# Blocks of 512 queries, a slot softmax behind the loop, and a list scheduler, in attention followed by a soft mixture of experts

## The chip, the cores and the metric

The kernel runs on one core of a Trainium2 chip. PE is TensorE (matrix products), DVE is VectorE, ACT is ScalarE, POOL is GpSimd, and SP issues DMA transfers. Each engine works through its own list of instructions in order and waits on semaphores for the others. The metric is the device time of one execution in microseconds (us), as the median of three runs.

## The reference

q has 4 batches of 12288 queries with 128 channels. Keys and values are the same 768 vectors per batch: kv pooled 4 by 4, times w_sr. Attention is followed by a soft mixture of experts with 32 slots (8 experts of 4):

```python
kv_flat = kv_pool.reshape(B, -1, C) @ w_sr      # k = v, 768 x 128 per batch
s = scale * (q @ k.transpose(0, 2, 1))
a = np.exp(s - s.max(-1, keepdims=True)); a /= a.sum(-1, keepdims=True) + 1e-09
x = (a @ v).reshape(B * N, C)                   # 49152 x 128
logits = x @ phi                                # 49152 x 32
d = softmax of logits over all rows             # dispatch
slot_out = experts(d.T @ x)                     # relu(. @ w1) @ w2
c = softmax of logits over the 32 slots         # combine
out = c @ slot_out
```

## The kernel before, in words

**Blocks and steps.** The queries go through in 192 blocks of 256. Of each block the scores are made transposed, 768 keys in six tiles of 128 on the partitions, queries along the free axis (`qk`, L289 to L291: three products per tile, since keys and queries are split into a high and a low part). The score tiles s lie in three PSUM tiles of one bank each, each with two buffers: six of the eight banks. The remaining two hold everything else (`pm`, tag m).

The row maximum crosses partitions. DVE takes a maximum of every 32 by 32 square while it transposes it (`rowmax1`, L301, result r), reduces over tiles (L309), multiplies by a pattern (L314, result rq), PE spreads this over the partitions (`rowmax_pe`, L322, result pq), DVE reduces again (L327) and transposes it into mb (L332). It subtracts mb from the scores into t in SBUF (`sub_part`, L342). ACT takes the exponential twice (L352 into 16-bit phi, L353 into 32-bit t), POOL subtracts the two into plo (L362), and PE multiplies phi and plo with the values and with values times the router phi (`av`, L377, L378, L380, result px; 161 columns: a row sum, 128 channels, 32 logits). ACT copies px into xl (L393). Query splits: ACT copies q into qhi, POOL makes qlo (L272), 512 queries at a time.

**Groups.** Every 2048 queries form a group (steps `g0` to `g7`): logits L, their running maximum mrun (L489), the weights D (POOL, L495 and L514) and the dispatch sum pd (PE, L555), added to acc with rescaling. The combine softmax is made per group, too (steps `k3`, `k5`, `k6`, `k8`): maximum and sum over slots on DVE (L477, L524), subtraction and multiplication on POOL (L480, L536), four transposes on PE (L567), copied into cT. The last 2048 queries are two small groups whose steps run on DVE.

**Batches.** Keys and values of the next batch are summed by accumulating transfers on POOL's queue, the last halves by POOL itself (`kv_fold`). PE makes K (pk) and V (pv), DVE klo.

**Order.** The order is written out by hand: PROG lists the steps of a block with lags, and group and batch steps are hung in at fixed block numbers. PE, DVE, ACT and POOL keep the order in which the program records.

**Behind the loop** come the experts (ph, pso), the split of the slot outputs, and the output: 25 chunks, each with 12 products on PE (po, L799), four evacuations on DVE and ACT, a high/low split (chi, clo) on ACT and POOL, and its transfer.

## Time and profile before

| what | value |
|---|---|
| median of 3 runs | 1234.87 us (1234.6 to 1235.92) |
| profiled execution: its time, its span | 1237.04 us, 1235.3 us |
| PE, DVE, POOL, ACT busy | 1119.8, 1093.4, 913.2, 859.1 us |
| granted TensorE clock, mean over the span | 0.983 |
| first scores, first expert product, first output product | 21.05, 1144.30, 1158.83 us |

The span runs from the first to the last instruction of the profiled execution; its time has what lies around it as well. Busy times of one engine are a union of its instructions. Ends of PE instructions are modelled, so the distance between starts says more of PE than durations do.

### The profile page before, as it was taken

To read this page: it belongs to the slowest core of one execution; us is meant where nothing else is said; L and a number is where in the kernel's file an instruction comes from. 1 tells how busy PE (TensorE), PEld (TensorE's weight loads), DVE (VectorE), ACT (ScalarE), POOL (GpSimd) and SP (SyncE) were. 2 spreads that over 40 slices of the span, in tenths; PEclk is the share of its full clock that TensorE was granted. 3 is DMA by queue.
4 is the path that set the end of the run, shared out by engine and by line. 5 is a ranking of instruction groups with operands and counts; after the bars stand their busy time and mean duration, and the time that the engine had idled before them with its cause. 6 is when DMAs were issued, how large, how long until landed. Compare 5 with 4: busy or idle time off the path is not lost.

```text
span 1235.3 us, 29414 instructions
## 1 busy us (share of the span) xinstructions
PE 1119.8 (91%) x12120; PEld 1062.9 (86%) x12120; DVE 1093.4 (89%) x2369; ACT 859.1 (70%) x1042; POOL 913.2 (74%) x498
## 2 busy tenths in 40 slices
PE   3799999988999999998999999998999999996897
PEld 2699989988989989988989999987989999996586
DVE  6899999988999999989999999889999999998454
ACT  1577777766777777866777777776777877775364
POOL 0478888976788888976888879966888778775242
PEclk9799999999999999999999999999999999999899
DMA  9113230210133220210132310210110110013398
GB/s 353 60 34 92 58 77 2 86 36 1 36 73 66 59 63 2 87 35 2 35 87 53 83 39 2 86 36 1 36 35 2 36 35 2 35 36 104 106 370 341
DMA packets 19446, 85.92 MB, mean 70 GB/s; under 512 B 1648, under 2 KB 7024, under 8 KB 13424
## 3 DMA queue, kind: packets, MB, share of 16 engines
q1 hardware_dynamic: 12064, 56.37, 12.8%
q0 software_dynamic: 2448, 14.16, 6.1%
q10 hardware_dynamic: 4800, 13.52, 2.8%
q8 instruction: 96, 1.57, 0.5%
q14 instruction: 38, 0.31, 0.1%
HBM read 58.87 MB, written 25.17 MB: 68 GB/s over the span
## 4 chain that ended last, share of the span: by engine, by line
PE 50%; DVE 43%; ACT 3%; issue 2%; DMA 1%; DVEq 0%; SPq 0%
DVE r L301 14%; DVE t L342 11%; PE px L380 9%; PE px L377 8%; PE px L378 8%; PE po L799 5%; PE s L289 4%; PE s L291 4%; PE s L290 4%; PE pq L322 3%; DVE mrun L489 2%; DVE rq L314 2%; DVE cm L455 2%; DVE mb L332 2%; PE pd L555 2%
## 5 line engine op out<-in xcount | busy, mean ns | idle before, releaser
L362 POOL TENSOR_TENSOR plo<-t,phi 128x1536 f16<-128x1536 f32 x192 | 602.9, 3140 | 185.0 <-ACT t L353 71.9
L301 DVE TRANSPOSE_TENSOR_REDUCE r<-s 128x16 f32<-128x512 f32 x576 | 406.5, 706 | 12.5 <-PE s L291 9.7
L342 DVE TENSOR_TENSOR t<-s,mb 128x512 f32<-128x512 f32 x576 | 362.1, 684 | 16.9
L377 PE MATMUL px<-vhi,phi 128*128 128x161 f16 x2304 | 360.8, 235 | 0.3 <-DVE c L469 0.3
L378 PE MATMUL px<-vlo,phi 128*128 128x160 f16 x2304 | 360.7, 234 | 0.0
L289 PE MATMUL s<-qhi,khi 128*128 128x256 f32 x1152 | 344.0, 299 | 6.0 <-DVE t L342 5.5
L290 PE MATMUL s<-qlo,khi 128*128 128x256 f32 x1152 | 325.8, 283 | 0.0
L291 PE MATMUL s<-qhi,klo 128*128 128x256 f32 x1152 | 325.2, 282 | 0.4 <-DVE klo L183 0.4
L352 ACT ACTIVATE phi<-t,lnk 128x1536 f16<-128x1536 f32 (+1 forms) x193 | 301.4, 1562 | 22.0 <-DVE t L342 22.0
L353 ACT ACTIVATE t<-t,lnk 128x1536 f32<-128x1536 f32 (+1 forms) x193 | 302.9, 1569 | 6.3
L393 ACT ACTIVATE xl<-px 128x322 f32<-128x322 f32 x192 | 84.5, 440 | 259.3 <-PE px L380 203.6
L377 PEld LDWEIGHTS <-phi 128*128 128x128 f16 x2304 | 242.4, 105 | 0.0
L380 PE MATMUL px<-vhi,plo 128*128 128x161 f16 x2304 | 230.7, 235 | 0.0
L289 PEld LDWEIGHTS s<-qhi,khi 128*128 128x128 f32 x1152 | 219.7, 191 | 12.3 <-issue 7.0
L378 PEld LDWEIGHTS <-phi 128*128 128x128 f16 x2304 | 226.5, 98 | 0.3 <-issue 0.3
L290 PEld LDWEIGHTS s<-qlo,khi 128*128 128x128 f32 x1152 | 219.7, 191 | 0.9 <-issue 0.7
L291 PEld LDWEIGHTS s<-qhi,klo 128*128 128x128 f32 x1152 | 219.3, 190 | 0.7 <-DVE klo L183 0.7
L380 PEld LDWEIGHTS <-plo 128*128 128x128 f16 x2304 | 176.9, 99 | 0.2 <-DVE plo L362 0.2
L272 POOL TENSOR_TENSOR qlo<-q,qhi 128x512 fp32r<-128x512 f32 x96 | 126.7, 1321 | 56.6 <-ACT qhi L270 56.6
L322 PE MATMUL pq<-rq,sel 128*128 128x32 f32 x384 | 73.2, 273 | 71.7 <-DVE rq L314 71.2
L322 PEld LDWEIGHTS pq<-rq,sel 128*128 128x128 f32 x384 | 57.6, 189 | 92.1 <-issue 34.6
L332 DVE STREAM_TRANSPOSE mb<-m 128x256 f32<-128x256 f32 x192 | 77.2, 402 | 0.0
(134 smaller groups left out, 1084.7 us busy)
## 6 DMA issues: line engine op xcount, KB each, us to landing
q<-qT SPq DMA_DIRECT2D x23, 1024.0 KB, 4.9
...
```

What stands on the lines that cost most here:

```text
L289: nc.tensor.matmul(s[:, t, :], khi[:, ks], hi[:, sl], start=True, stop=False)
L290: nc.tensor.matmul(s[:, t, :], khi[:, ks], lo[:, sl], start=False, stop=False)
L291: nc.tensor.matmul(s[:, t, :], klo[:, ks], hi[:, sl], start=False, stop=True)
L301: nc.vector.tensor_reduce(out=MX[i][:, t0 : t0 + n, :], in_=S[i][h].rearrange("p t (b j) -> p t b j", j=Q32), axis=X, op=ALU.max, apply_tr ...
L322: nc.tensor.matmul(pqv, sel, MX[i].rearrange("p k b -> p (k b)"), start=True, stop=True)
L342: nc.vector.tensor_tensor(out=t[:, t0 : t0 + n, :], in0=S[i][k], in1=m.unsqueeze(1).broadcast_to([P, n, BQ]), op=ALU.subtract)
L352: nc.scalar.activation(hi[:, k : k + n, :], tk, AF.Exp, bias=lnk, scale=SCALE)
L353: nc.scalar.activation(tk, tk, AF.Exp, bias=lnk, scale=SCALE)
L362: (nc.vector if k else nc.gpsimd).tensor_tensor(out=lo[:, sl, :], in0=t[:, sl, :], in1=PP[i][:, sl, :], op=ALU.subtract)
L377: nc.tensor.matmul(px3[:, k, :], hi[:, t, ks], vhi[:, t, :], start=(t == 0), stop=False)
L378: nc.tensor.matmul(px3[:, k, 1:], hi[:, t, ks], vlo[:, t, :], start=False, stop=False)
L380: nc.tensor.matmul(px3[:, k, :], lo[:, t, ks], vhi[:, t, :], start=False, stop=(t == NT - 1))
```

## The change

**Blocks and tiles.** A block has 512 queries, so there are 96 of them. The three score tiles have two banks each and one buffer. One DVE instruction takes a maximum over two banks (1024 elements a partition), and subtractions are 1024, 512, 512 and 1024 wide, since t is now made of half blocks of three key tiles (three buffers). Exponentials and plo work on a half block: the same size as before (128 x 1536), and as many of them. The two remaining banks m0 and m1 are handed out by the planner; pq and its small result use the top columns of a bank beside px. Query splits are 512 wide as before, one for each block.

**Planner.** Each step is recorded with an engine, a cost, a due time, its dependencies and the buffers that it takes. `Plan.emit` then simulates the engines and writes out the steps: at each engine it takes, of what could start within 0.12 us, the step with the smallest due time; steps of the row maximum are marked hot and go first.

**Moved work.** The combine softmax keeps all logits in LL and runs group by group, but its steps depend on the last subtraction of the loop (end_) and have the last due times. The transposes read LL by chunk, in the output stage, and clo is made by DVE, straight from PSUM. `kv_fold` is two accumulating transfers instead of POOL's additions. The group maximum is taken with one transposing reduction, and gm stays in PSUM. The last group pair is 1536 and 512 queries. All output transfers go through SP. The first query load has 512 columns, as before, but this is now one block.

```diff
+AVD = 2.0
+HOLD = 0.7
+URGE = 60.0
...
+        def best(e):
+            found = []
+            for n in avail[e]:
+                t = acquire(n, free[e])
+                if t is not None:
+                    found.append((max(free[e], ready[n], t), ops[n][3], n))
+            if not found:
+                return None
+            t0 = min(found)[0] + 0.12
+            hot = [f for f in found if ops[f[2]][9]]
+            if hot:
+                h = min(hot)
+                if h[0] - t0 < HOLD:
+                    fits = [(p, t, n) for t, p, n in found if t <= t0 and t + ops[n][1] <= h[0] + 0.1]
+                    return min(fits) if fits else (h[1], h[0], h[2])
+            return min((p, t, n) for t, p, n in found if t <= t0)
...
-    BQ = 256
+    BQ = 512
...
+    NH = 2
+    TH = NT // NH
+    PB = 5
+    TBUF = 3
...
-    ps = es.enter_context(tc.tile_pool(name="ps", bufs=2, space=PSUM))
-    pm = es.enter_context(tc.tile_pool(name="pm", bufs=2, space=PSUM))
+    ps = es.enter_context(tc.tile_pool(name="ps", bufs=1, space=PSUM))
+    pm = es.enter_context(tc.tile_pool(name="pm", bufs=1, space=PSUM))
...
+    LL = cp.tile([P, NB * TB, NS], F32, tag="LL", name="LL")
+    RM = cp.tile([P, NB * TB], F32, tag="RM", name="RM")
...
+    banks = [pm.tile([P, 512], F32, tag=f"m{b}", name=f"m{b}") for b in range(2)]
+
+    def mt(shape, name):
+        return banks[plan.bank]
...
     def kv_fold(b, h):
-        yield POOL_
         t = kvs[b]
-        if h == 0:
-            nc.gpsimd.tensor_tensor(out=t[:, 0:2, :], in0=t[:, 0:2, :], in1=t[:, 2:4, :], op=ALU.add)
-        else:
-            pooled[b] = bp.tile([P, NK], F32, tag="pooled", name=f"pooled_{b}", bufs=1)
-            nc.gpsimd.tensor_tensor(out=pooled[b], in0=t[:, 0, :], in1=t[:, 1, :], op=ALU.add)
...
+        n = 2 - h
+        nc.gpsimd.dma_start(out=t[:, :n, :], in_=t[:, n : 2 * n, :], accum_op=ALU.add, max_dma_last_dim=4 * 2 * NK)
+        if h:
+            pooled[b] = t[:, 0, :]
...
+    def qk(i, t):
+        khi, klo = kT[i // BPB]
+        hi, lo = qsp[i]
+        if t % 2 == 0:
+            S[i, t // 2] = ps.tile([P, 2, BQ], F32, tag=f"s{t // 2}", name=f"s_{i}_{t // 2}")
+        s = S[i, t // 2][:, t % 2, :]
+        ks = slice(t * P, (t + 1) * P)
+        nc.tensor.matmul(s, khi[:, ks], hi, start=True, stop=False)
+        nc.tensor.matmul(s, khi[:, ks], lo, start=False, stop=False)
+        nc.tensor.matmul(s, klo[:, ks], hi, start=False, stop=True)
...
+    def rowmax1(i, u):
+        if u == 0:
             MX[i] = sp.tile([P, NT, NBK], F32, tag="r6", name=f"r6_{i}")
-        t0, n = SG[h]
         nc.vector.tensor_reduce(
-            out=MX[i][:, t0 : t0 + n, :], in_=S[i][h].rearrange("p t (b j) -> p t b j", j=Q32), axis=X,
+            out=MX[i][:, 2 * u : 2 * u + 2, :].rearrange("p t b -> p (t b)"),
+            in_=S[i, u].rearrange("p t (b j) -> p (t b) j", j=Q32), axis=X,
             op=ALU.max, apply_transpose=True,
         )
...
+        top = banks[plan.bank][:, 512 - (NQD + 1) * NBK :]
+        pq = PQ[i] = top[:, NBK:]
+        r1 = top[:, :NBK]
...
+    def sub(i, t, n):
+        h, o = divmod(t, TH)
+        if o == 0:
+            TT_[i, h] = sp.tile([P, TH, BQ], F32, tag="t", name=f"t_{i}_{h}", bufs=TBUF)
+        u = t % 2
         nc.vector.tensor_tensor(
-            out=t[:, t0 : t0 + n, :], in0=S[i][k], in1=m.unsqueeze(1).broadcast_to([P, n, BQ]), op=ALU.subtract
+            out=TT_[i, h][:, o : o + n, :], in0=S[i, t // 2][:, u : u + n, :],
+            in1=MX[i].unsqueeze(1).broadcast_to([P, n, BQ]), op=ALU.subtract,
         )
...
+        d["gm"] = d["pc"][:, NS : 2 * NS]
         nc.vector.transpose(out=d["gm"], in_=c1.broadcast_to([P, NS]))
...
+    def k_max(g):
+        o, n = GB[g][0] * TB, nt(g)
+        nc.vector.tensor_reduce(out=RM[:, o : o + n], in_=LL[:, o : o + n, :], axis=X, op=ALU.max)
...
+        o, n = GB[g][0] * TB, nt(g)
+        c = LL[:, o : o + n, :]
+        nc.gpsimd.tensor_tensor(out=c, in0=c, in1=bc(RM[:, o : o + n], NS), op=ALU.subtract)
...
+    def k_rec(g):
+        o, n = GB[g][0] * TB, nt(g)
+        r = RM[:, o : o + n]
+        nc.vector.tensor_scalar_add(r, r, EPS)
+        nc.vector.reciprocal(out=r, in_=r)
...
+        if n == 3:
+            ops["qr", 0] = op("SP", 0.5, 28.0, 0, [loaded[-1]], lambda: q_load(0, BQ, GQ))
...
+        pe = op("PE", 0.27, 0.3, T0 - 10, [r2], lambda i=i: rowmax_pe(i), use=[("m", ("pq", i)), ("rq", i)], hot=True)
...
+        for t, n in ((0, 2), (2, 1), (3, 1), (4, 2)):
...
+        a = op("DVE", dve(n), 0.08, p, [ops["L", g]] + end_, lambda g=g: k_max(g))
+        a = op("POOL", n / 512, 0.1, p, [a, ops["g4", g]], lambda g=g: k_sub(g))
+        a = op("ACT", act(n), 0.1, p, [a], lambda g=g: k_exp(g))
+        a = op("DVE", dve(n), 0.08, p, [a], lambda g=g: k_sum(g))
+        a = op("DVE", 0.3, 0.08, p, [a], lambda g=g: k_rec(g), raw=0.14)
+        ops["c", g] = op("POOL", n / 512, 0.1, p, [a], lambda g=g: k_mul(g))
...
+    def c_t(g):
+        o, n = chunks[g]
+        pt = U[g, "pt"] = mt([P, 512], f"pt_{g}")
+        for j in range(n):
+            k = (o + j) * TS
+            nc.tensor.transpose(out=pt[:, j * P : (j + 1) * P], in_=LL[:, k : k + TS, :], identity=ident)
...
+    def c_lo(g):
+        n = chunks[g][1] * P
+        nc.vector.tensor_tensor(out=U[g, "lo"], in0=U[g, "pt"][:, :n], in1=U[g, "hi"].bitcast(F32), op=ALU.subtract)
```

**PE around the row maximum** (m is one of the two shared banks, pq in it; phi, plo: the block two steps back). Before, the end of a block's scores:

```order
L290 MATMUL s_4_9418<-qlo_9097,khi_8141 128x256
L291 MATMUL s_4_9418<-qhi_9096,klo_8142 128x256
L322 MATMUL pq_9404<-rq_9406,sel 128x32 [waits DVE_49,PE_49]
L377 LDWEIGHTS phi_9198
L377 MATMUL px_9426<-vhi_8724,phi_9198 128x161 [waits Activation_49]
```

and after, in block 53, where 30 px matmuls stand between the scores and these rows:

```order
L528 LDWEIGHTS phi_1_7357
L528 MATMUL m_113<-vlo_6004,phi_1_7357 128x160
L479 MATMUL m_112<-rq_7560,sel 128x64 [waits DVE_49,Activation_49]
L535 LDWEIGHTS plo_0_7410
L535 MATMUL m_113<-vhi_6003,plo_0_7410 128x161
```

pq moved from the end of the scores (of the block before, by lag) to behind one and two thirds of the four px tiles of the same turn.

**POOL at the start.** Before:

```order
L272 TENSOR_TENSOR qlo_126<-q_111,qhi_125 128x512
L272 TENSOR_TENSOR qlo_208<-q_111,qhi_207 128x512
L272 TENSOR_TENSOR qlo_210<-q_111,qhi_209 128x512
L362 TENSOR_TENSOR plo_295<-t_258,phi_269 128x1536
L272 TENSOR_TENSOR qlo_311<-q_111,qhi_310 128x512
```

and after:

```order
L442 TENSOR_TENSOR qlo_133<-q_117,qhi_132 128x512
L512 TENSOR_TENSOR plo_0_248<-t_0_234,phi_0_242 128x1536
L512 TENSOR_TENSOR plo_1_251<-t_1_240,phi_1_246 128x1536
L442 TENSOR_TENSOR qlo_254<-q_117,qhi_253 128x512
L442 TENSOR_TENSOR qlo_257<-q_117,qhi_256 128x512
```

The second query split now stands behind both plo of the first block; the planner gives the transfer that it reads (`ops["qr", 0]`) 28 us.

**DVE in the experts.** Before, the steps follow each other (som, so: sums over slot outputs):

```order
L724 TENSOR_SCALAR hs<-ph_18077 128x512
L738 COPY hT<-pht_18097 128x4x16
L738 COPY hT<-pht_18104 128x4x16
L766 TENSOR_TENSOR som_18132<-pso_18119,mask 128x512
L770 TENSOR_REDUCE so_18122<-som_18132 128x128
```

and after, the moved softmax (LL, RM) lies between them:

```order
L992 TENSOR_SCALAR hs<-ph 128x512
L1007 COPY hT<-m_113 128x4x16 x2
L674 TENSOR_REDUCE RM<-LL 128x16
L1007 COPY hT<-m_112 128x4x16 x2
L688 TENSOR_REDUCE RM<-LL 128x16 x2
L693 TENSOR_SCALAR RM<-RM 128x16
L694 RECIPROCAL RM<-RM 128x16
L1020 TENSOR_TENSOR som_14018<-pso,mask 128x512
```

Four softmax steps and more stand in front of som that were not there.

More of the change, by code (lines that the diff above doesn't have):

```diff
@@ L463, in g3, with g2q, g3m @@
+        nc.vector.tensor_reduce(out=cm, in_=d["L"], axis=X, op=ALU.max, apply_transpose=True)
+        d["cmt"] = sm2(g, "cmt", [P, 1])
+        nc.vector.tensor_reduce(out=d["cmt"], in_=cm, axis=X, op=ALU.max)
+    def g2q(g):
+        d = G[g]
+        d["cq"] = sm2(g, "cq", [P, NQD])
+        scale(g, d["cq"], quad, d["cmt"])
+    def g3m(g):
+        pc = G[g]["pc"] = mt([P, 512], f"pc_{g}")
+        nc.tensor.matmul(pc[:, :NQD], sel, G[g]["cq"], start=True, stop=True)
     def g3(g):
         d = G[g]
-        pc = pm.tile([P, 512], F32, tag="m", name=f"pc_{g}")
@@ L680, in advance @@
-    def advance(jobs, phase):
-        for j in jobs:
-            while j[1] is not None and j[1] <= phase:
-                j[1] = next(j[0], None)
-    for i in range(LAST):
-        jobs = []
-        for f, a in work.pop(i, []):
-            r = f(*a)
-            if r is not None:
-                jobs.append([r, PE_])
-        for name, d in PROG:
-            if name[0] == "J":
-                advance(jobs, int(name[1]))
-            elif 0 <= i - d < NB:
-                if i == 0 and name == "Q2":
-                    run(kv_k(0, 1))
-                STEP[name](i - d)
@@ L698, in attention_then_soft_moe @@
-    assert not work
-    ER = E // NQD
-    psi = pm.tile([P, 512], F32, tag="m", name="psi")
-    nc.tensor.matmul(psi[:, :NS], acc[:, 1 : C + 1], sel1, start=True, stop=True)
-    nc.tensor.matmul(psi[:, NS : NS + 1], sel, acc[:, :1], start=True, stop=True)
-    for r in range(ER):
-        src = psi[:, r * NQD * SE : (r + 1) * NQD * SE].rearrange("p (j k) -> p j k", k=SE)
-        dst = sm[:, r * NQD : (r + 1) * NQD, r * SE : (r + 1) * SE]
-        if r:
-            nc.scalar.activation(dst, src, AF.Copy)
-        else:
-            nc.vector.tensor_copy(dst, src)
@@ new lines, in act, with start_q, start_kv @@
+    def act(n, aps=0):
+        return n / 1200 + 0.08 + 0.093 * aps
+    last = {}
+    LAND = 1.46
+    def start_q():
+        q_load(0, 0, BQ)
+    def start_kv(which):
+        kv_load(which)
+    ops = {}
+    ops["q", 0] = op("SP", 0.5, 9.5, 0, [], start_q, acq=[("q", 0)])
+    LOADS = ([(0, 0, 6)], [(0, 6, 6)], [(0, 12, 4), (1, 0, 4)], [(1, 4, 12)])
+    lands = {}
+    at = 6.5
+    for h in range(2):
+        for c in range(0, R2, 2):
+            lands[h, c] = at
+            at += LAND if h == 0 else LAND / 2
@@ L754, in attention_then_soft_moe, with t_psi @@
[L754 to L760 removed]
+    U = {}
+    HF = NF // 2
+    W = {}
+    def t_psi():
+        psi = W["psi"] = mt([P, 512], "psi")
+        nc.tensor.matmul(psi[:, :NS], acc[:, 1 : C + 1], sel1, start=True, stop=True)
+        nc.tensor.matmul(psi[:, NS : NS + 1], sel, acc[:, :1], start=True, stop=True)
@@ new lines, in t_so, with t_q @@
+    def t_so(h):
+        W["so", h] = cp.tile([P, C], F32, tag=f"so{h}", name=f"so_{h}")
+        nc.vector.tensor_reduce(out=W["so", h], in_=W["som", h].rearrange("p e c -> p c e"), axis=X, op=ALU.add)
+    def t_q():
+        W["psq"] = ps.tile([P, 2, 512], F32, tag="s2", name="psq")[:, 0, :]
+        for h in range(2):
+            nc.tensor.matmul(W["psq"][:, :C], sel, W["so", h], start=(h == 0), stop=(h == 1))
+        W["sz"] = bp.tile([P, NK], F32, tag="pooled", name="sz", bufs=1)
+        W["shi"] = bp.tile([P, NK], F32R, tag="khi", name="shi")
+        W["slo"] = bp.tile([P, NK], F32R, tag="klo", name="slo")
```

983 lines of the change are left out of this document (578 added, 405 removed), and 4 rows, old and new, of the table PROG.

## The prediction

> **What bounds the kernel now.** I read the page first: how busy each engine is, and the chain that ended last.
>
> ```profile
> span 1235.3 us, 29414 instructions
> PE 1119.8 (91%) x12120; PEld 1062.9 (86%) x12120; DVE 1093.4 (89%) x2369; ACT 859.1 (70%) x1042; POOL 913.2 (74%) x498
> PE 50%; DVE 43%; ACT 3%; issue 2%; DMA 1%; DVEq 0%; SPq 0%
> ```
>
> PE and DVE share the chain almost evenly. So they hand work to each other, and neither bounds it alone. The windows show that this holds through the main loop, and that the output stage is different: there PE alone is full. The third row counts the instructions that touch the tile mb.
>
> ```profile
> 300.00:600.00 300.00, 278.33 (x3183) 269.64 (x3183) 279.39 (x611) 222.95 (x262) 242.24 (x130) 1.00 0.18 47
> 600.00:900.00 300.00, 280.46 (x3225) 271.75 (x3223) 278.22 (x611) 221.40 (x263) 241.55 (x128) 0.99 0.17 44
> 300.00:900.00 600.00, 239.04 (x419) 1.00 0.17 45
> 1180.00:1200.00 20.00, 20.00 (x88) 16.10 (x87) 9.92 (x16) 12.21 (x23) 9.45 (x9) 1.00 0.91 373
> ```
>
> Each block of 256 queries touches mb four times (one transpose, three subtractions), so 419/4 = 104.75 blocks pass in 600 us: 5.73 us a block, 11.46 us per 512 queries. DVE is busy for 557.6 of the 600 us, 10.65 us per 512 queries. Next is one block on DVE, from one row maximum to the next:
>
> ```profile
> 609.45 0.72 DVE L301 TRANSPOSE_TENSOR_REDUCE r<-s 128x16 f32<-128x512 f32 x1
> 610.09 0.21 DVE L309 TENSOR_REDUCE pq<-r 128x8 f32<-128x48 f32 x1
> 610.34 0.19 DVE L314 TENSOR_TENSOR rq<-pq,quad 128x32 f32<-128x32 f32 x1
> 610.45 0.70 DVE L301 TRANSPOSE_TENSOR_REDUCE r<-s 128x16 f32<-128x512 f32 x1
> 611.10 0.19 DVE L327 TENSOR_REDUCE m<-pq 128x8 f32<-128x32 f32 x1
> 611.20 0.70 DVE L301 TRANSPOSE_TENSOR_REDUCE r<-s 128x16 f32<-128x512 f32 x1
> 611.83 0.40 DVE L332 STREAM_TRANSPOSE mb<-m 128x256 f32<-128x256 f32 x1
> 612.34 1.89 DVE L342 TENSOR_TENSOR t<-s,mb 128x512 f32<-128x512 f32 x3
> 614.39 0.72 DVE L301 TRANSPOSE_TENSOR_REDUCE r<-s 128x16 f32<-128x512 f32 x1 [0.17 <-PE s L291]
> ```
>
> Starts count here, not durations, since ends overlap: 0.64 for a maximum, 0.25, 0.11 and 0.10 for the small steps, 0.51 for the transpose, about 0.60 for each subtraction. That is 4.7 us a block, 9.4 per 512. The other 10.65 - 9.4 = 1.25 us is work per group of 2048 queries and per batch. PE over one block:
>
> ```profile
> 602.48 1.09 PE L555 MATMUL pd<-xl,D 128*32 128x129 f32 x32
> 603.50 0.39 PE L289 MATMUL s<-qhi,khi 128*128 128x256 f32 x1
> 603.72 0.28 PE L290 MATMUL s<-qlo,khi 128*128 128x256 f32 x1
> 605.61 0.28 PE L291 MATMUL s<-qhi,klo 128*128 128x256 f32 x1
> 605.75 0.38 PE L322 MATMUL pq<-rq,sel 128*128 128x32 f32 x2
> 605.96 0.23 PE L377 MATMUL px<-vhi,phi 128*128 128x161 f16 x1
> 608.46 0.36 PE L289 MATMUL s<-qhi,khi 128*128 128x256 f32 x1
> ```
>
> The 36 matmuls of px take 608.46 - 605.96 = 2.50 us, 0.0694 each. Scores come every (605.61 - 603.72)/16 = 0.118 us, with 0.10 more for the first; pq takes 0.21 and pd 1.02.
>
> **The loop after the change.** 512 queries need the same 72 px matmuls (5.00 us) and 18 score matmuls of 512 columns instead of 36 of 256. The output stage has that width; 51 matmuls lie between these two starts:
>
> ```profile
> 1165.24 0.40 PE L799 MATMUL po<-chi,shi 128*128 128x512 f32 x1
> 1177.14 0.40 PE L799 MATMUL po<-chi,shi 128*128 128x512 f32 x1
> ```
>
> 11.90/51 = 0.233 us, twice 0.118: wide blocks save PE nothing in the scores, 18 x 0.233 = 4.20, plus 0.10. One pq of 64 columns replaces two (0.28, an estimate from 0.21). Per group pd 1.02 and pc about 0.3 remain, 0.33 a block; the four batches' K and V products I take at 0.11 a block. **PE needs 10.0 us per block.**
>
> DVE gains from fewer starts. Slope and fixed part come from two sizes of one form; the others price what follows.
>
> ```profile
> L352 ACT ACTIVATE phi<-t,lnk 128x1536 f16<-128x1536 f32 x191 | 299.6, 1568 | 22.0 <-DVE t L342 22.0
> L804 DVE COPY o<-po 128x512 f32<-128x512 f32 x46 | 31.8, 691 | 30.4 <-PE po L799 29.8 <-ACT o L802 0.6
> L804 DVE COPY o<-po 128x256 f32<-128x256 f32 x4 | 1.7, 424 | 1.2 <-PE po L799 0.9 <-ACT o L802 0.3
> L524 DVE TENSOR_REDUCE cs<-c 128x16 f32<-128x512 f32 x23 | 15.8, 685 | 7.2 <-ACT c L521 7.2
> L536 POOL TENSOR_TENSOR c<-c,cs 128x512 f32<-128x512 f32 x23 | 24.2, 1051 | 0.0
> ```
>
> (691 - 424)/256 = 1.04 ns an element, so 512 more cost 0.53 us. Three maxima: 3 x 1.17 = 3.51; small steps 0.30 + 0.14 + 0.13; transpose 0.78; subtractions 2 x 1.13 + 2 x 0.60 = 3.46; sum 8.3 instead of 9.4. The moved slot softmax takes two reductions and a reciprocal out of each group, about 1.4 us or 0.35 a block. The running maximum mrun becomes cheaper too:
>
> ```profile
> 1121.97 3.11 POOL L362 TENSOR_TENSOR plo<-t,phi 128x1536 f16<-128x1536 f32 x1 [1.78 <-ACT t L353]
> 1123.06 2.08 DVE L489 TENSOR_TENSOR mrun<-mrun,gm 128x32 f32<-128x32 f32 x1
> 1135.84 0.19 DVE L489 TENSOR_TENSOR mrun<-mrun,gm 128x32 f32<-128x32 f32 x1
> ```
>
> With POOL in plo it lasts until plo ends (1125.1); with POOL idle it takes 0.19. Both inputs lie in SBUF now; the change leaves gm in PSUM, as rq's input is, and rq never shows such a wait. I take 0.2 instead of about 1.4, 0.3 a block less. DVE: 8.3 + 1.25 - 0.35 - 0.3 = 8.9 us. ACT keeps four exponentials of 1.57 us, and POOL loses the moved multiplications and the fold: both stay below 9 (POOL is at 81% of 11.46 = 9.2 now). **So PE becomes the longer engine**; 11.46 falls towards 10.0.
>
> What isn't hidden: score tiles now have one buffer, so each block is a loop through both engines. Scores end at 4.3 us, the last maximum can start at 4.5, rq is there at about 6.3. PE reaches pq after 30 px matmuls, 4.3 + 2.1 = 6.4: no wait, but no slack either. Behind pq on PE stand the remaining 42 px matmuls and the next scores. The first subtraction ends at 8.8, before PE needs the tile at 9.6. DVE work that comes in between (group work, 2.4 us in four blocks) makes rq late and PE wait; DVE regains up to 2 x (1.40 - 1.17) = 0.46 a block, as maxima stop waiting for scores. px tile 2 also takes pq's bank and waits for its reader, about 0.1. Ends: 10.0 (all hidden) and 10.7 (none). I take 10.3, nearer the low end since 4 x 0.46 covers most of the 2.4. 92 blocks (the 4th to the 95th) last **948 us**. At the three changes of batch, scores are split around px tiles and wait for klo: 0 to 5 us each, taken as **7.5 us**.
>
> **Start.** Now the next query splits precede plo on POOL; in the change qlo of block 1 stands behind both plo of block 0.
>
> ```profile
> 21.05 0.61 PE L289 MATMUL s<-qhi,khi 128*128 128x256 f32 x1
> 31.47 2.50 POOL L272 TENSOR_TENSOR qlo<-q,qhi 128x512 fp32r<-128x512 f32 x2 [19.33 <-ACT qhi L270]
> 36.71 1.89 DVE L342 TENSOR_TENSOR t<-s,mb 128x512 f32<-128x512 f32 x3
> ```
>
> The first subtractions, twice as wide, end at about 41.5 instead of 38.6. The last of four exponentials ends at 46, the second plo at 46 + 3.1, qlo at 50.5. Blocks 1 and 2 then run the loop with little px work, 9 to 10 us each: block 3 scores at **70 us**, against 21 + 3 x 10.3 = 52 without that order. Bounds 60 and 74.
>
> **Behind the loop.** Three starts of now, the last subtractions among them:
>
> ```profile
> 1120.68 1.89 DVE L342 TENSOR_TENSOR t<-s,mb 128x512 f32<-128x512 f32 x3
> 1144.30 6.32 PE L722 MATMUL ph<-w,sm 128*32 128x512 f32 x32 [0.27 <-DVE sm L710]
> 1158.83 0.50 PE L799 MATMUL po<-chi,shi 128*128 128x512 f32 x1 [0.79 <-ACT shi L779]
> 1117.59 0.60 PE L567 MATMUL pt<-ident,c 128*128 128x128 f32 x4
> ```
>
> Now 36.3 us pass from the last subtraction (1122.5) to the first output. After the change the last block's subtractions end **12 us** behind its first score. Its exponentials, two plo and four px tiles put the last px about 8 us later than now. Until the expert products DVE also carries 23 slot reductions (0.65), 8 reciprocals with their additions (0.45) and 5 clo (0.65): 22 us, of which I count 5 unhidden, and 4 more between the expert products and the output: 36.3 + 8 + 5 + 4 = **53 us**, bounds 45 and 70.
>
> Output lasts 1235.3 - 1158.8 = 76.5 us. The chunk transposes now lie inside it, 20 of 25 beyond the five made ahead, 0.6 us each, on the engine that is full: **88.5 us**. Two evacuations and a clo per chunk (1.9 us on DVE) hide under PE's 3.4.
>
> Sum: 70 + 948 + 7.5 + 12 + 53 + 88.5 = 1179 us of span. The profiled execution took 1237.0, 1.7 more than its span; the median of the runs, 1234.9, is 0.4 less than the span. **Forecast 1178 us**, 4.6% less than now.
>
> **Rivals.** *PE alone sets the loop.* All DVE work is hidden and a block takes 10.0: 92 x 0.28 = 26 less, 1152 us. For it: the list order puts small DVE steps into waits for pq. Against it: rq arrives with 0.1 to spare.
>
> *DVE's port in the tail.* The mrun rows show DVE held by POOL for up to a whole instruction. Behind the loop POOL runs some 50 instructions of 1.05 us back to back, while DVE makes 25 additions on RM and some 25 small steps of the last groups in SBUF. At 0.5 us each half of these 50 lie on the path and half are hidden: 12 us, and 8 more if the reductions queued behind delay the output's evacuations: 20 more, 1198 us. Against it: not every form waits. The Trainium skill, "SBUF — State Buffer", section "SBUF: two separate sides", says that DVE and GpSimd hold their shared port pair as an exclusive lock for a whole instruction, for DVE operations in a two-port mode or with two SBUF inputs. By that rule these additions wait; the mrun rows agree.
>
> *POOL's queue holds the subtractions: slower.* Tile t becomes three half blocks, so the second half of a block's subtractions waits for plo of the previous block's first half. In every fourth block POOL has D in front of that plo, and D's second step waits for an exponential behind both phi on ACT. I put that plo at 18.8 us after that block's first score, and the subtraction at 19.9: 1.1 us spare. Each microsecond beyond costs 24 groups x 1 us. It decides from 2.4 us of stall per group; with 3 us, 24 x 3 = 72 more, 1250 us. Against it: ACT and POOL have over 1 us a block free.
>
> **How the numbers follow.** Forecast 0.52 (its own range 1160 to 1197), PE alone 0.22, the port 0.17, POOL's queue 0.06; 0.03 for something that leaves no difference. Range 1140 to 1212: it takes in the first three, with the unknown period (10.0 to 10.5) and tail. What a measurement can tell from no change is about 0.2%. Faster 0.91, same 0.03, slower 0.06.
>
> **What would show it.** Right: a score block every 10.2 to 10.4 us, PE the longest engine, mrun near 0.2 us, scores of block 3 near 70 us, 3.4 us per output chunk. Wrong: PE waiting for pq over 0.5 us in most blocks (DVE still sets the pace), DVE subtractions waiting for POOL, or over 60 us between the last subtraction and the first output. The forecast fails if 512-column scores on DVE cost more than 1.2 us each, since rq is late at once.

## The result and the profile after

The changed kernel takes **1202.0 us** (median of four runs, 1200.8 to 1203.3) against 1234.7 us for the kernel before on the same chip. The ratio is 0.9736, 95% interval 0.9719 to 0.9752: 2.6% faster. The forecast was 1178 us, so the sign and the range held, and 24 us of the expected gain are missing. The page of the changed kernel: span, busy time by engine, chain of work that ended last.

```profile
span 1199.1 us, 24770 instructions
PE 1101.0 (92%) x10200; PEld 941.9 (79%) x10200; DVE 1028.8 (86%) x1555; ACT 817.2 (68%) x989; POOL 867.4 (72%) x473
PE 61%; DVE 32%; ACT 3%; issue 2%; DMA 1%; POOL 1%; DVEq 0%; SPq 0%; ACTq 0%; POOLq 0%
```

PE's share of the chain went from 50% to 61%. The windows (span, then busy time of PE, PEld, DVE, ACT, POOL, then clock, DMA share, GB/s) say the same stage by stage:

```profile
300.00:600.00 300.00, 293.43 (x2864) 256.39 (x2862) 266.81 (x383) 225.38 (x262) 244.30 (x127) 0.99 0.20 51
1160.00:1180.00 20.00, 17.96 (x85) 13.57 (x82) 11.11 (x17) 9.10 (x17) 0.00 (x0) 1.00 0.64 263
```

In the loop PE is busy for 97.8%, up from 93%. In the output stage it is the other way round: PE was full there before (20.00 of 20) and now has 17.96. Next the transposes into mb, one per block, in a stretch without work for a new batch: number, durations, first and last start. The first row is of the kernel before (blocks of 256), the second of the changed one.

```profile
L332 DVE STREAM_TRANSPOSE mb<-m x33: 400/402/404, 583.5 to 761.1; 128x256 f32<-128x256 f32 x33
```

```profile
L489 DVE STREAM_TRANSPOSE mb<-m x21: 711/711/712, 765.4 to 968.3; 128x512 f32<-128x512 f32 x21
```

Before: 177.6/32 = 5.55 us per 256 queries, 11.10 per 512. Now: 202.9/20 = **10.15 us per block**, and PE hardly waits in it. Its wait for rq over the 16 blocks from 800 to 960 us (us in total, times, longest):

```profile
PE m L479 <- DVE rq L471: 0.7, 4, 0.2
```

The landmarks of the changed kernel, from its timeline: scores of block 3, scores of the last block, its last subtractions, first output product.

```profile
66.85 0.64 PE L452 MATMUL s<-qhi,khi 128*128 128x512 f32 x1 [2.48 <-DVE t L497]
...
1032.14 0.48 PE L452 MATMUL s<-qhi,khi 128*128 128x512 f32 x1
...
1042.22 2.41 DVE L497 TENSOR_TENSOR t<-s,mb 128x512 f32<-128x512 f32 x3
...
1101.55 0.80 PE L1076 MATMUL po<-chi,shi 128*128 128x512 f32 x1 [1.30 <-ACT shi L1042]
```

| stage | predicted us | measured us | how measured | miss |
|---|---|---|---|---|
| start to scores of block 3 | 70 | 66.9 | row above | -3 |
| 92 blocks, without K and V | 92 x 10.19 = 938 | 92 x 10.15 = 934 | mb rows | -4 |
| K and V for three new batches, rest of the loop | 7.5 + 10 | 31 | 1032.1 - 66.9 - 934 | +14 |
| last block to the end of its subtractions | 12 | 12.5 | 1044.6 - 1032.1 | 0 |
| to the first output product | 53 | 57 | 1101.6 - 1044.6 | +4 |
| output | 88.5 | 97.5 | 1199.1 - 1101.6 | +9 |

The forecast's 10.3 us a block holds 0.11 us for PE's K and V products. The mb rows come from a stretch without them, so these 92 x 0.11 = 10 us stand in the third row. The sum of the misses is the 20 us of span between 1179 and 1199. Against the kernel before: the last subtraction ends 78 us earlier (1122.5 to 1044.6), the way from there to the output is 21 us longer (36.3 to 57), and the output is 21 us longer (76.5 to 97.5). More than half of what the loop gained was given back behind it.

**Where the loop loses 31 us.** From mb to mb, groups of four blocks last 40.1 to 41.2 us, but the three that prepare K and V of the next batch last 49.8, 51.0 and 49.8 us, 9.2, 10.4 and 9.2 more than 40.6: 28.8 of the 31 us. DVE in the first of them (timeline; two rows of POOL between):

```profile
218.97 0.71 DVE L489 STREAM_TRANSPOSE mb<-m 128x512 f32<-128x512 f32 x1
...
224.69 0.29 DVE L377 TENSOR_SCALAR dg<-ident,am 128x128 f32<-128x128 f32 x1
...
225.24 6.37 POOL L512 TENSOR_TENSOR plo<-t,phi 128x1536 f16<-128x1536 f32 x2 [4.47 <-DVE am L374]
225.28 3.17 DVE L377 TENSOR_SCALAR dg<-ident,am 128x128 f32<-128x128 f32 x1
228.37 2.37 DVE L459 TRANSPOSE_TENSOR_REDUCE r<-s 128x32 f32<-128x1024 f32 x2
231.08 0.54 DVE L389 TENSOR_SCALAR g<-g 128x2 f32<-128x2 f32 x1
231.56 1.27 POOL L442 TENSOR_TENSOR qlo<-q,qhi 128x512 fp32r<-128x512 f32 x1
231.66 1.19 DVE L390 TENSOR_SCALAR g<-g 128x2 uint32<-128x2 uint32 x1
...
233.32 1.19 DVE L459 TRANSPOSE_TENSOR_REDUCE r<-s 128x32 f32<-128x1024 f32 x1
...
236.81 0.71 DVE L489 STREAM_TRANSPOSE mb<-m 128x512 f32<-128x512 f32 x1
```

This one block lasts 17.84 us. The scaled identity dg takes 0.29 us once and 3.17 us the second time, when POOL has just begun plo; a step on two columns takes 1.19 us beside POOL's qlo. Both dg stand ahead of all three maxima of the block, the steps on g ahead of the third. PE in the same stretch:

```profile
218.99 1.08 PE L362 MATMUL m<-w_sb,kva 128*128 128x160 f32 x6
...
220.73 1.08 PE L362 MATMUL m<-w_sb,kva 128*128 128x160 f32 x6 [0.23 <-ACT v L365]
221.54 0.50 PE L452 MATMUL s<-qhi,khi 128*128 128x512 f32 x1
...
228.59 0.67 PE L381 MATMUL m<-dg,ones 128*128 128x256 f32 x2 [0.69 <-DVE dg L377]
...
235.85 0.41 PE L479 MATMUL m<-rq,sel 128*128 128x64 f32 x2 [2.06 <-DVE rq L471]
```

From 218.99 to 221.54 PE makes parts of V and K, 2.3 us without the wait. With the first part of K (0.86 us before these rows) and the product with dg (0.32 us) a preparation is 3.5 us of PE's own work. In these four blocks PE waits 4.9 us: 2.4 for rq, 0.9 for ACT's xl, 0.7 for a subtraction, 0.7 for dg, 0.2 for V. So of the 9.2 us about 3.5 are products and about 5 are waits.

**Where the output loses 9 us.** One chunk, PE and DVE (timeline):

```profile
1140.10 1.39 DVE L1084 COPY o<-po 128x512 f32<-128x512 f32 x2 [1.32 <-PE po L1076]
...
1140.60 0.60 PE L1053 MATMUL m<-ident,LL 128*128 128x128 f32 x4
...
1141.54 0.50 PE L1076 MATMUL po<-chi,shi 128*128 128x512 f32 x1 [0.34 <-DVE o L1084]
```

The product at 1141.54 goes into the second bank of a po tile whose first bank DVE empties until 1141.49, and PE waits for that copy. In the kernel before, every po tile had one bank; the two-bank tile came with the change. The product at the same place one chunk earlier starts at 1137.69: 3.85 us a chunk, not 3.4.

**Theories.** From here on the theory was: PE sets the steady block, and the missing 24 us are the K and V work (DVE held by POOL, ahead of the maxima) and the two-bank output tile. The main rivals: DVE or the ring of single score buffers sets the block; the amount of DVE work, not its place or its waits, makes the losses.

### The profile page after: what moved, and what is told of

It is laid out like the page before. It is cut to its first block, busy times and chain, and to the rows that moved or that the text cites. A ratio compares the mean times of both kernels' runs of the same rounds, so it can differ in the third digit from the quotient of the medians.

```text
span 1199.1 us, 24770 instructions
## 1 busy us (share of the span) xinstructions
PE 1101.0 (92%) x10200; PEld 941.9 (79%) x10200; DVE 1028.8 (86%) x1555; ACT 817.2 (68%) x989; POOL 867.4 (72%) x473
## 4 chain that ended last, share of the span: by engine, by line
PE 61%; DVE 32%; ACT 3%; issue 2%; DMA 1%; POOL 1%; DVEq 0%; SPq 0%; ACTq 0%; POOLq 0%
PE m L527 9%; PE m L528 9%; PE m L535 9%; DVE t L497 8%; PE s L452 8%; PE s L453 8%; PE s L454 8%; DVE r L459 8%; PE po L1076 5%; PE m L479 3%; DVE o L1084 2%; DVE mb L489 2%; PE m L663 2%; DVE cm L601 1%; ACT phi L504 1%
## 5 line engine op out<-in xcount | busy, mean ns | idle before, releaser
L504 ACT ACTIVATE phi<-t,lnk 128x1536 f16<-128x1536 f32 x192 | 301.5, 1570 | 149.2 <-DVE t L497 147.6
L459 DVE TRANSPOSE_TENSOR_REDUCE r<-s 128x32 f32<-128x1024 f32 x288 | 352.0, 1237 | 37.8 <-PE s L454 30.9
L527 PE MATMUL m<-vhi,phi 128*128 128x161 f16 x2304 | 361.5, 235 | 12.2 <-ACT phi L504 8.4
L528 PE MATMUL m<-vlo,phi 128*128 128x160 f16 x2304 | 360.8, 234 | 0.0
L497 DVE TENSOR_TENSOR t<-s,mb 128x1024 f32<-128x1024 f32 (+1 forms) x384 | 343.6, 950 | 8.0
L508 ACT ACTIVATE t<-t,lnk 128x1536 f32<-128x1536 f32 x192 | 299.8, 1568 | 2.9
L452 PE MATMUL s<-qhi,khi 128*128 128x512 f32 x576 | 238.4, 414 | 5.8 <-DVE t L497 5.8
L535 PE MATMUL m<-vhi,plo 128*128 128x161 f16 x2304 | 230.4, 235 | 3.2 <-POOL plo L512 3.2
L454 PE MATMUL s<-qhi,klo 128*128 128x512 f32 x576 | 229.3, 398 | 0.5 <-DVE klo L350 0.5
L453 PE MATMUL s<-qlo,khi 128*128 128x512 f32 x576 | 229.3, 398 | 0.1
```

The source lines that it names most:

```text
L452: nc.tensor.matmul(s, khi[:, ks], hi, start=True, stop=False)
L453: nc.tensor.matmul(s, khi[:, ks], lo, start=False, stop=False)
L454: nc.tensor.matmul(s, klo[:, ks], hi, start=False, stop=True)
L459: nc.vector.tensor_reduce(out=MX[i][:, 2 * u : 2 * u + 2, :].rearrange("p t b -> p (t b)"), in_=S[i, u].rearrange("p t (b j) -> p (t b) j" ...
L497: nc.vector.tensor_tensor(out=TT_[i, h][:, o : o + n, :], in0=S[i, t // 2][:, u : u + n, :], in1=MX[i].unsqueeze(1).broadcast_to([P, n, BQ ...
L504: nc.scalar.activation(hi, TT_[i, h], AF.Exp, bias=lnk, scale=SCALE)
```

## Experiments on the losses

All kernels here differ from the changed kernel by the edit whose main lines the diff shows; costs and steps in the planner's list go with it. Times are medians, and their ratios to the kernel before come from runs on one chip; the changed kernel's own ratio is 0.9736.

The experiments ran on other chips than the changed kernel, and the kernel before took 1236.0 to 1237.6 us there instead of 1234.7. So differences between medians are off by up to 3 us. By the ratios the experiments on the losses are, in the order below, 16, 5, 12 and 12 us less, 2 us more and 10 us less than the changed kernel; those on mrun and on narrow maxima are 5 and 10 us more. The stages behind the loop also differ by 3 us where no edit touches them: tail and output together last 154 us in the changed kernel and 157 and 158 us in the experiments on the start and on dg. Why is not known. Where it matters, the loop is therefore read by itself: from the scores of block 3 to those of block 95 it lasts 965.3 us (1032.1 - 66.9).

**One copy per output tile.** Pair 0 of each chunk goes through DVE, pair 1 through ACT; the step is recorded for t = 1 and 3 only, and the first chunk is sent out in two parts instead of four.

```diff
-        src = U[g, "po", t // 2][:, t % 2, :n].rearrange("p (j q) -> p j q", q=P)
-        if t % 2:
-            nc.scalar.activation(U[g, "o"][:, :, t, :], src, AF.Copy)
+        src = U[g, "po", t // 2][:, :, :n].rearrange("p t (j q) -> p j t q", q=P)
+        dst = U[g, "o"][:, :, t - 1 : t + 1, :]
+        if t // 2:
+            nc.scalar.activation(dst, src, AF.Copy)
         else:
-            nc.vector.tensor_copy(U[g, "o"][:, :, t, :], src)
+            nc.vector.tensor_copy(dst, src)
```

> Output stage only: each two-bank tile po is emptied by one 1024-column copy (pair 0 of a chunk on DVE, pair 1 on ACT) instead of one 512-column copy per bank. In the changed kernel a chunk of output lasts 3.85 us (1141.54 - 1137.69), not the 3.4 us of its 12 products and four transposes; PE stands 0.35 us per chunk behind DVE's copy. My theory: the two banks are one tile, so the copy of bank 0 waits for the products of bank 1 and the products of bank 1 wait for a copy; with one copy per tile this ring opens, PE is full at 3.4 us, 25 x 0.45 = 11 us less: 1191 us, no wait of PE for DVE in the chunks. Rival: DVE and ACT or the output transfers set the 3.85 us; then the copies (1.22 + 0.69 us of DVE per chunk, the same sum as now) change nothing: 1202 us.

Measured: **1188.0 us**, ratio 0.9609 (0.9593 to 0.9625), 14 us less than the changed kernel. Its output stage, windows first, then two starts of one place in the timeline:

```profile
1140.00:1160.00 20.00, 20.00 (x101) 16.34 (x100) 10.94 (x12) 10.23 (x14) 0.00 (x0) 1.00 0.78 318
```

```profile
1143.12 0.48 PE L1076 MATMUL po<-chi,shi 128*128 128x512 f32 x1
...
1144.10 1.23 DVE L1085 COPY o<-po 128x1024 f32<-128x1024 f32 x1 [1.42 <-PE po L1076]
...
1146.37 0.48 PE L1076 MATMUL po<-chi,shi 128*128 128x512 f32 x1
```

PE is full, without a wait for DVE, and a chunk lasts 3.25 us. The ring through the tile was the loss. It cost more than the 11 us expected, since the transposes of a chunk take PE 0.35 us and not the 0.6 us that the prediction had: without the ring the output lasts 83.4 us (1102.8 to 1186.2), 14 less than 97.5.

**K and V work three blocks later.**

```diff
-            kv_ops(nb, T0 + 15 * PER, [[f1], [f1]], dep)
+            kv_ops(nb, T0 + 18 * PER, [[f1], [f1]], dep)
```

> One number: the K and V work for the next batch gets due times three blocks later (18 instead of 15 periods behind its base), so in the list order it gives way to the blocks' own work and fills gaps. In the changed kernel the four blocks that hold this work last 49.8, 51.0 and 49.8 us against 40.6 elsewhere: 9.2, 10.4 and 9.2 us for the three, where the prediction had 7.5 for all. Theory 'order': its DVE steps (about 9.7 us each time, 4 of them waits for POOL's plo) stand ahead of the maxima of one block and hold up its pq; as gap work half or more is hidden: 5 to 7 us of each, 1184 us. Rival 'amount': DVE and PE have no gap left, the work costs the same three blocks later: 1200 to 1204 us.

Measured: 1198.3 us, ratio 0.9692 (0.9675 to 0.9710): 4 us less, far from the theory's 1184 and just below the rival's 1200. One block still takes 17.5 us, with dg again at 3.16 us beside plo. A later due time doesn't spread the steps: the list takes them in one run again, three blocks on. So the rival is much the closer here: the place is worth 1.2 us of each preparation on average (loop 961.4 us).

**dg on ACT, g in PSUM.** The three steps that follow the maximum work on h; the last of them writes g to SBUF.

```diff
-        nc.vector.tensor_scalar_mul(dg[:, k, :], ident, am[:, k : k + 1])
+        nc.scalar.activation(dg[:, k, :], ident, AF.Copy, scale=am[:, k : k + 1])
...
-        nc.vector.tensor_reduce(out=g, in_=pa2, axis=X, op=ALU.max)  
+        h = pa[:, 2 * P : 2 * P + 2]
+        nc.vector.tensor_reduce(out=h, in_=pa2, axis=X, op=ALU.max)
```

> K and V work for the next batch: the scaled identity dg is made on ACT instead of DVE, and the three small steps on g write and read a PSUM bank instead of SBUF; nothing else. In the changed kernel, in each of the three preparations, the second dg lasts 3.17 us instead of 0.29 and two steps on g 0.54 and 1.19 instead of 0.17, each until POOL's running plo or qlo ends; the preparations cost 9.2 to 10.4 us each. Theory 'port': these 4.3 us are DVE held by POOL, as mrun was; they leave, since ACT and the PSUM operand do not wait: 3 x 4 = 12 us less, 1190 us. Rival 'amount': what holds pq is the chain of products, copies and maxima with an extra hop to ACT; then 1199 to 1203 us.

Measured: **1192.7 us**, ratio 0.9640 (0.9615 to 0.9664): 9 us less. DVE in the same block:

```profile
226.34 1.25 DVE L464 TRANSPOSE_TENSOR_REDUCE r<-s 128x32 f32<-128x1024 f32 x1 [0.93 <-PE s L459]
...
229.45 0.17 DVE L394 TENSOR_SCALAR m<-m 128x2 f32<-128x2 f32 x1
229.65 0.17 DVE L395 TENSOR_SCALAR m<-m 128x2 uint32<-128x2 uint32 x1
229.85 0.16 DVE L396 TENSOR_SCALAR g<-m 128x2 f32<-128x2 f32 x1
```

```profile
229.77 3.10 POOL L517 TENSOR_TENSOR plo<-t,phi 128x1536 f16<-128x1536 f32 x1 [0.93 <-ACT t L513]
```

The steps that took 0.54 and 1.19 us take 0.17. POOL stands still beside these two, in all three preparations, so they don't show what an operand in PSUM is worth; the third step, with its input in PSUM, does: 0.16 us beside plo. The maxima no longer stand behind dg, and the three groups of four blocks last 46.6, 46.4 and 46.4 us: 5.8 us each above 40.6 instead of 9.6. So 11 of 29 us went with DVE's waits for POOL and the two dg that left DVE. Of the remaining 5.8 us, 3.4 are PE's own products; PE's waits have fallen from 4.9 to 1.8 us.

**Rest of the first query load due earlier.**

```diff
-            ops["qr", 0] = op("SP", 0.5, 28.0, 0, [loaded[-1]], lambda: q_load(0, BQ, GQ))
+            ops["qr", 0] = op("SP", 0.5, 14.0, 0, [loaded[-1]], lambda: q_load(0, BQ, GQ))
```

> One number: the planner takes the rest of the first query load as landed 14 us after its issue instead of 28 (the trace shows 7.1), so the query splits of block 1 stand ahead of both plo of block 0 on POOL. Theory: block 1 scores at about 34 us (first subtraction of block 0 ends at 33.7) instead of 45.4; then tile t waits for plo of block 0, which ends as before, so part is lost again: block 3 at about 58 instead of 66.9, 9 us less, 1193 us. Rival: plo and the exponentials of block 0 fix when block 1's subtractions can go, block 3 scores at 66 as before: 1202 us.

Measured: **1190.9 us**, ratio 0.9638 (0.9623 to 0.9652): 11 us less. First scores of blocks 1 and 3 (timeline):

```profile
34.26 0.77 PE L452 MATMUL s<-qhi,khi 128*128 128x512 f32 x1 [2.67 <-DVE t L497]
...
56.06 0.48 PE L452 MATMUL s<-qhi,khi 128*128 128x512 f32 x1
```

Block 3 scores at 56.1 instead of 66.9 us. One number in the planner, a landing time of 28 us where the trace shows 7.1, cost 11 us, because the order written from it is fixed.

**The slot softmax in the loop again.**

```diff
-        a = op("DVE", dve(n), 0.08, p, [ops["L", g]] + end_, lambda g=g: k_max(g))
+        a = op("DVE", dve(n), 0.08, p, [ops["L", g]], lambda g=g: k_max(g))
```

> Undoes one part of the change: the slot softmax of a group no longer waits for the last block's subtractions, but may run in the loop, at the lowest priority of the list (the chunk transposes still wait for the end). Tail now: 57 us from the last subtraction (1044.6) to the first output product (1101.6), DVE full in it with 24 x (0.60 + 0.60 + about 0.4) = 38 us of slot softmax. Theory: the loop has gaps on DVE (0.8 us a block) and POOL, at lowest priority most is hidden there; the tail falls to about 42 us, the loop grows by up to 5 us: 1192 us. Rival (what the change assumes): each step in the loop delays a block by its length, 24 x 1.6 = 38 us, and the tail gives back 15: 1225 us.

Measured: 1205.3 us, ratio 0.9751 (0.9737 to 0.9766): 3 us more than the changed kernel by the medians, 2 by the ratios, whose intervals overlap. Its mb rows in the loop, then its last subtractions and first output product:

```profile
L489 DVE STREAM_TRANSPOSE mb<-m x21: 711/711/712, 768.1 to 973.0; 128x512 f32<-128x512 f32 x21
```

```profile
972.15 0.68 DVE L674 TENSOR_REDUCE RM<-LL 128x16 f32<-128x512 f32 x1
...
1057.28 2.41 DVE L497 TENSOR_TENSOR t<-s,mb 128x512 f32<-128x512 f32 x3
...
1106.10 0.79 PE L1076 MATMUL po<-chi,shi 128*128 128x512 f32 x1 [0.79 <-ACT shi L1042]
```

The tail falls to 46.4 us (1059.7 to 1106.1), 10.5 less, not the 15 of both theories; a steady block takes 204.9/20 = 10.25 us, 0.1 more, and the last transpose into mb comes 15 us later in all. The row at 972.15 stands where DVE used to wait for pq, and fills that wait, but others stand ahead of a maximum. The addition to the sums (L693) is one of these, and it lasts 1.08 us in the median here and 0.16 us at the least. Whether the softmax would pay in the loop without that addition was not tried. Moving the softmax behind the loop, taken alone, gains 2 to 3 us, which the intervals don't separate from nothing.

**The tail without DVE's small scalings.** The first edit is in `scale`, the addition in `k_rec`, the last in the steps behind the loop.

```diff
-        if g >= FAST:
-            nc.vector.tensor_scalar_mul(out, in_, by)
-        else:
-            nc.scalar.activation(out, in_, AF.Copy, scale=by)
+        nc.scalar.activation(out, in_, AF.Copy, scale=by)
...
-        nc.vector.tensor_scalar_add(r, r, EPS)
...
-        nc.vector.tensor_scalar_mul(qt, quad, tsum)
+        nc.scalar.activation(qt, quad, AF.Copy, scale=tsum)
```

> Behind the loop only: the small scalings of the last two groups and qt go to ACT, and the addition of 1e-9 to the sums of the slot softmax is left out (these sums are at least 1, so no output changes). In the changed kernel DVE is full from the last subtraction (1044.6) to the first output product (1101.6), and small steps in it last far longer than their own time beside POOL's running multiplications: 3.07, 1.09 and 1.09 us for scalings of 12 and 4 columns, up to 0.86 us for the additions, 1.13 us for qt; about 9 us of such waits in all. Theory 'port' (the rival of the prediction, in part): the 57 us fall by 8 to 10 us, 1193 us. Rival 'amount': DVE's 38 us of reductions and the chain set the tail, and ACT's hops cost what the waits gave: 1199 to 1203 us.

Measured: 1194.4 us, ratio 0.9657 (0.9642 to 0.9672): 8 us less. What the small steps cost can be seen in the timeline of the changed kernel, DVE and POOL together:

```profile
1044.55 4.83 DVE L674 TENSOR_REDUCE RM<-LL 128x16 f32<-128x512 f32 x8
1046.38 3.12 POOL L512 TENSOR_TENSOR plo<-t,phi 128x1536 f16<-128x1536 f32 x1
...
1050.66 3.10 POOL L512 TENSOR_TENSOR plo<-t,phi 128x1536 f16<-128x1536 f32 x1
1050.72 3.07 DVE L556 TENSOR_SCALAR ru<-r,g 128x12 f32<-128x12 f32 x1
```

Twelve columns take as long as POOL's plo. In this experiment the scaling is on ACT, and the wait goes to the next step that reads two operands from SBUF:

```profile
1052.73 2.70 DVE L590 TENSOR_TENSOR LL<-xl,ru 128x384 f32<-128x384 f32 x1
...
1096.04 0.79 PE L1072 MATMUL po<-chi,shi 128*128 128x512 f32 x1 [1.41 <-ACT shi L1038]
```

That step has 384 columns and took 0.55 us in the changed kernel. Still, the tail falls from 57 to 50 us (1045.9 to 1096.0), of which up to 3 us are the additions' own time (16 of the 25 lie in the tail, 0.11 to 0.17 us each where they don't wait).

## Experiments on what sets the block

**Less work for PE, less work for DVE.** Two kernels, with one run each and so no interval. In the first, `av_lo` keeps one product of six:

```diff
-        for t in range(NT):
-            nc.tensor.matmul(px, PP[i, t // TH][1][:, t % TH, ks], vhi[:, t, :], start=False, stop=(t == NT - 1))
+        nc.tensor.matmul(px, PP[i, 1][1][:, TH - 1, ks], vhi[:, NT - 1, :], start=False, stop=True)
```

> Leaves out 20 of the 24 products with plo per block (5 of 6 per px tile), so part of the attention sum is missing; PE's work falls from 10.0 to 8.6 us per block, all else stays. Theory 'PE sets the block': the steady block falls from 10.15 us towards DVE's 9.35 us of work: 9.4 to 9.6 us, about 1143 us. Rival 'the ring sets it' (scores, maxima, pq, first subtraction, next scores, one buffer each): the steady block stays near 10.1 us, 1198 us. Third: with PE out of the way the ring alone, 8.9 us: not below DVE's 9.35.

In the second, `rowmax1` and `rowmax2` leave out the first two key tiles:

```diff
+        if u == 0:
+            return
...
-        nc.vector.tensor_reduce(out=r1, in_=MX[i].rearrange("p t b -> p b t"), axis=X, op=ALU.max)
+        nc.vector.tensor_reduce(out=r1, in_=MX[i][:, 2:, :].rearrange("p t b -> p b t"), axis=X, op=ALU.max)
```

> Leaves out the row maximum of the first two key tiles of every block (one of three wide maxima; the shift of the exponentials then comes from the other four tiles): DVE's work falls from 9.35 to 8.1 us per block, all else stays. Theory 'PE sets the block': 10.15 falls only to PE's 10.0 to 10.05 us, 8 to 14 us less, 1190 us. Rival 'DVE or the ring sets it': each block falls by up to 1.2 us, at most to PE's work, which the rival puts below 9.5: 1140 us or less.

Measured: 1165.9 us with less for PE, 1191.3 us with less for DVE. The mb row of the first, and one window:

```profile
L489 DVE STREAM_TRANSPOSE mb<-m x21: 711/712/714, 762.5 to 954.9; 128x512 f32<-128x512 f32 x21
```

```profile
300.00:600.00 300.00, 271.38 (x2401) 227.16 (x2399) 275.83 (x402) 237.07 (x275) 257.06 (x134) 0.98 0.26 64
```

The same two views of the second:

```profile
L491 DVE STREAM_TRANSPOSE mb<-m x21: 711/712/714, 768.3 to 969.4; 128x512 f32<-128x512 f32 x21
```

```profile
300.00:600.00 300.00, 294.04 (x2910) 259.07 (x2910) 237.40 (x358) 225.64 (x263) 247.27 (x129) 0.99 0.22 55
```

With 1.4 us less for PE the block falls to 192.4/20 = 9.62 us, with DVE busy for 92% and PE for 90%: no engine is full any more, PE waits for rq and for ACT's xl, and 0.53 us below 10.15 was all the room there was. With 1.2 us less for DVE it falls only to 201.1/20 = 10.06 us. **PE sets the steady block; DVE has about half a microsecond to spare**, and hiding all of DVE would bring 0.1 us a block. The total of the first run missed its 1143 us by 23. Half of that is the block, 9.62 instead of 9.5 us; the other half is that the preparations cost about 12 us more there than in the changed kernel (loop 928.7 us, where 92 x 0.53 less would be 916.5). The four runs of the changed kernel differ by 2.5 us; these two times are 36 and 11 us below its median.

**mrun's input in SBUF again.**

```diff
-        d["gm"] = d["pc"][:, NS : 2 * NS]
+        d["gm"] = sm2(g, "gm", [P, NS])
```

> Undoes one part of the change: the group maximum gm lies in SBUF again instead of PSUM. mrun took 1.41 us on average before and takes 0.19 now. My prediction counted this as 0.3 us of DVE per block. Theory A: DVE holds the path at that step (it stands between a block's subtractions), so each of 24 groups loses the 1.2 us: 29 us more, 1231 us. Theory B: PE is the longer engine (97.8% busy) and DVE regains most of it before pq is due: 0 to 10 us more, 1202 to 1212 us; mrun itself is long again in both.

Measured: 1209.6 us, ratio 0.9777 (0.9755 to 0.9799): 8 us more than the changed kernel by the medians, 5 by the ratios, as the second theory had it. The group of mrun in the changed kernel, and in this one:

```profile
L624 DVE TENSOR_TENSOR mrun<-mrun,m 128x32 f32<-128x32 f32 x24 | 4.5, 188 | 0.8
```

```profile
L624 DVE TENSOR_TENSOR mrun<-mrun,gm 128x32 f32<-128x32 f32 x24 | 13.2, 548 | 0.8
```

The wait is back, but at 0.36 us on average instead of 1.2 before the change. POOL is in plo or qlo in 21 of the 24 groups, but in 13 of them mrun starts only 0.3 us before plo ends. The steady block stays at 10.15 (21 rows of mb from 762.7 to 965.7 us). The loop lasts 971.3 us, 6 more, in the preparations and some groups; the rest of the 8 us lies ahead of the loop and behind it, where this edit changes next to nothing.

**Narrow maxima.**

```diff
-        nc.vector.tensor_reduce(
-            out=MX[i][:, 2 * u : 2 * u + 2, :].rearrange("p t b -> p (t b)"),
-            in_=S[i, u].rearrange("p t (b j) -> p (t b) j", j=Q32), axis=X,
-            op=ALU.max, apply_transpose=True,
-        )
+        for k in range(2):
+            nc.vector.tensor_reduce(
+                out=MX[i][:, 2 * u + k, :], in_=S[i, u][:, k, :].rearrange("p (b j) -> p b j", j=Q32),
+                axis=X, op=ALU.max, apply_transpose=True,
+            )
```

> Undoes one part of the change: each of the three row maxima over a two-bank tile is made in two instructions of 512 columns, as before the change. Two narrow ones start 0.64 us apart (1.28 us), a wide one lasts 1.17 to 1.27 us, so DVE gets 0.1 to 0.3 us more per block. Theory A (PE sets the block and DVE has about 0.5 us free): steady block 10.15 to 10.2 us, 1200 to 1207 us, and the maxima of the first bank can even start earlier. Theory B (a later rq makes PE wait at once, as my prediction held): 93 x 0.3 = 28 us more, 1230 us.

Measured: 1214.8 us, ratio 0.9819 (0.9800 to 0.9838): 13 us more by the medians, 10 by the ratios, between the two. A steady block takes 0.1 us more:

```profile
L489 DVE STREAM_TRANSPOSE mb<-m x21: 711/711/714, 764.5 to 969.4; 128x512 f32<-128x512 f32 x21
```

204.9/20 = 10.25. So DVE's time isn't all hidden either: what makes rq late is paid for in part even while PE is the longer engine. The loop lasts 975.3 us, so the wide maxima are worth 10 of the 78 us by which the last subtraction came earlier.

**All four together.** The first three gains and the tail in one kernel; then with the later K and V work as well.

> Four changes at once on the changed kernel: one copy per two-bank tile in the output (alone 14 us less), the query splits of block 1 ahead of plo of block 0 (11 less), dg on ACT and g in PSUM (9 less), the tail without DVE's small scalings (8 less by my theory). They lie in four stages one behind another. Theory: they add up, 1202 - 14 - 11 - 9 - 8 = 1160 us. Rival: the list order shifts as a whole with each change and gives part back: 1165 to 1175 us.

> The four changes together, and the K and V work for the next batch three blocks later as well (alone 4 us less, each of three preparations 1.5 us cheaper). Theory: with DVE's waits for POOL gone the later place still saves 1 to 1.5 us each: 1156 us if the four alone give 1160, 3 to 4 us less than them. Rival: what the later place saved was part of those waits: no difference to the four alone.

Measured: **1158.3 us**, ratio 0.9368 (0.9354 to 0.9382), and 1158.6 us, ratio 0.9369 (0.9355 to 0.9383), with the later place. A window of the first:

```profile
300.00:600.00 300.00, 295.94 (x2922) 258.85 (x2921) 267.11 (x388) 228.40 (x270) 250.53 (x130) 1.00 0.25 61
```

The four gains add up by the medians (1202 - 14 - 11 - 9 - 8 = 1160); by the ratios they are 50 us singly and 45 together, a difference within what their intervals allow. The later place adds nothing once DVE's waits are gone, as the rival had it. PE is busy for 98.6% of the window. This kernel beats both: 3.6% below the changed kernel, 6.3% below the one before.

## Why the prediction was right or wrong

- **PE becomes the longer engine: right.** The sum had 10.3 us a block, 10.19 of it without K and V products, and a steady block takes 10.15. It is made up differently: PE needs 10.0 to 10.1 us, as the run with less for DVE shows (10.06), where I had 9.9, and it waits 0.05 us a block (0.7 us in 16 blocks), where I had 0.3. The two misses nearly cancel, so that the term fits so well is in part luck. "PE alone sets the loop", the first rival, is the better picture of the steady blocks, but its 1152 us are wrong for the same reasons as the forecast: the K and V work and the output.
- **"At the three changes of batch ... 0 to 5 us each, taken as 7.5": wrong by 14 us, the largest miss.** I priced the scores' wait for klo, and PE doesn't wait for klo at these places at all. PE's own products for K and V were right (0.11 a block is 3.4 us a preparation, 3.5 measured). What is missing is PE's other waits, 4.9 us in the first preparation, half of them for rq. Ahead of rq stands DVE's work on klo, am, dg and g; with vlo behind it this is 9.7 us of DVE time, of it 4.3 held by POOL. The DVE sum had such work only as a mean over all blocks, where it hides under PE; in one block it does not. The kernel before paid the same (from its block 36 to block 48, 75.9 us instead of 12 x 5.55 = 66.6), and it could have been read there: the 11.46 us I started from were a mean over 600 us that held two such preparations, and its steady value was 11.10.
- **Output, "two evacuations and a clo hide under PE's 3.4": wrong by 9 us.** The sign named for being right, 3.4 us per chunk, did not come: it is 3.85. The durations were right; that both banks of po belong to one tile, so that products and copies wait for each other, I did not look at, though the code of the change shows it. The 9 us are a difference of two misses: the ring costs 14 us, and the transposes are about 5 us cheaper than I had them.
- **Start: right.** 66.9 against 70 us, bounds 60 to 74, and for the reason given: with qlo ahead of plo, block 3 comes 11 us earlier (I had put that at 18).
- **Tail: 57 against 53 us, bounds 45 to 70.** The rival of DVE's port named a wait that is there: taking small steps off DVE gave 7 us of tail. It isn't the 20 us of the rival, since not every form waits and part of the wait only moves. The output lost its 9 us to the ring of the po tile, not to evacuations queued behind reductions, as the rival had it.
- **mrun: the step right, its worth not.** It lasts 0.19 us as predicted. I counted 0.3 us of DVE a block, 28 us in all; undoing it costs 5 to 8 us, and nothing in steady blocks.
- **POOL's queue holds the subtractions: did not happen.** No wait of DVE for POOL's plo shows in the steady blocks; groups of four without K and V work last 40.1 to 41.2 us throughout.

So the steady loop came out within 4 us of the forecast, and 23 us were lost in two places, the K and V work and the output tile. The step that failed is the same in both: I had not asked who waits for whom there.
